# A one-core decode layer: the last weight row in two loads, the last projection's columns in two PSUM banks with a store each, and the residual put into the banks first

## The chip, the cores and the metric

The kernel runs on one core of a Trainium2 chip. The metric is the device time of one execution in microseconds. Three runs of the kernel before gave 137.87, 137.88 and 137.82 us, a median of 137.87 us.

## What is computed

One decode step of a transformer layer for a batch of four tokens: layer norm, attention over the last 2048 positions of a key and value cache (32 query heads on 4 key/value heads), an output projection with a residual, a second layer norm, a gated feed-forward network, and a second residual. Everything enters and leaves in bf16.

```python
# x 4x1x1024; k_cache, v_cache 4x4x8192x128; wq 1024x4096; wo 4096x1024
# w1, w3 1024x3584; w2 3584x1024
h = x + attention(layernorm(x), k_cache, v_cache, wq, wo)   # window: the last 2048 positions
n = layernorm(h)
gate = n @ w1
up = n @ w3
h2 = h + (silu(gate) * up) @ w2
return h2
```

## The kernel before

With four tokens there is little arithmetic for each weight, so the kernel is a stream of 55.6 MB out of HBM through a ring of 160 KB in each of the 128 partitions. `plan` is the list of loads in order: wq, the keys, the values, wo, w1, w3, w2. Each entry has a place in the ring. `load_next(n)` issues the next `n` of them on the sync engine's DMA queue (SP); where it is called in the program decides after which matmuls the issue may come, since a load overwrites ring space that earlier matmuls read.

A "row" of a weight is one slice of the contraction: partition p of `w2_v` holds the 28 rows of w2 that belong to it one behind the other, and `loaded["w2"][i]` is row i in all partitions, 128 x 1024 values, 256 KB. The 28 rows of w2 come in four loads: rows 0 to 16, 17 to 23 (`R1` = 17), 24 to 26 (`R2` = 24) and row 27. The last three are issued by `load_next(3)` within the w1 matmuls (line 467).

Matrix products put the four tokens in a small stationary operand, 32 columns wide, and stream the weights. The 1024 output columns are cut into `JG` = 4 column groups of `CG` = 256; group j has its results in PSUM partitions 32j to 32j+31 (`QD` = 32), of which every eighth (`RS` = 8) belongs to a token. Four matmuls, one for each group, run at the same time in different columns of the array.

The work around the change, in program order:

- wo (L411): 32 rows into `y_ps`. VectorE adds the residual (L424) and has `h1`, the layer's middle value, 128 x 256 in fp32.
- The second layer norm (L426 to L449): statistics of `h1` on VectorE, one matmul that adds them over the column groups (L433, `sums_ps`), a square root on ScalarE, and the normalised rows transposed to `hnT`.
- w1 and w3 (L459, in `gate_up`): 64 matmuls each into `g_ps` and `u_ps`, with the silu on ScalarE and VectorE between; `hgT` (L481) is the transposed product.
- w2 (L492, in `down`): rows 0 to 16 go into the bank of `y2_ps`, whole groups of 256 columns. When they are done, VectorE adds `h1` and has `h2` (L501). Rows 17 to 27 go into two other banks, `ya_ps` with the first 128 columns of each group and `yb_ps` with the second 128 columns. Behind row 23 two matmuls with the fp32 identity `ident_f` add `h2` into these banks (L507).
- The end: VectorE copies `ya_ps` to bf16 (L513), ScalarE copies `yb_ps` (L514), and one DMA, issued on ScalarE's queue, stores all four column groups (L515). L541 is the end of the program, where the engines wait for all transfers and for one another.

The tile framework places the waits and may order independent instructions of an engine; the order of the queues quoted below is that of the built program.

Of the kernel before, what the change touches and what calls it, by code (L numbers as in the profile page):

```python
# [10 lines left out]
P = 128  # L11
ACT = mybir.ActivationFunctionType
ALU = mybir.AluOpType
AX = mybir.AxisListType
BF16 = mybir.dt.bfloat16
FP32 = mybir.dt.float32
# [3 lines left out]
def kernel(  # L20
# [13 lines left out]
    nc = tc.nc  # L34

    B, _, D = A_x.shape
# [13 lines left out]
    out_flat = out.flatten_outer_dims()  # L50
# [8 lines left out]
    wide = ctx.enter_context(tc.tile_pool(name="wide", bufs=2))  # L59
    const = ctx.enter_context(tc.tile_pool(name="const", bufs=1))  # L60
    act = ctx.enter_context(tc.tile_pool(name="act", bufs=1))
# [3 lines left out]
    JG = 4  # L65
    QD = P // JG
    RS = QD // B
    CQ = Hq * Dh // JG
    CG = D // JG
# [3 lines left out]
    IF = F // P  # L73
# [5 lines left out]

    RING = 5 * 16384  # L80
    R1, R2 = 17, 24
    RQ = 4
    BS = 2
    wq_v = A_wq.rearrange("(p i) n -> p (i n)", i=KC)
# [3 lines left out]
    w2_v = B_w2.rearrange("(p i) n -> p (i n)", i=IF)  # L88
    ring = stream.tile([P, RING], BF16)
# [33 lines left out]
    def load_tail(at, src, n, r0, m):  # L123

        t = ring[:, at : at + m * n]
        nc.sync.dma_start(out=t[:, : m * n - CE], in_=src[:, r0 * n : (r0 + m) * n - CE])
        return [t[:, k * n : (k + 1) * n] for k in range(m)]
    KIB = 512
    plan = [
        ("wq", load_rows, (0, wq_v, N_Q, 0, 4)),  # L130
        ("side", load_side, SETS[0]),
        ("side", load_side, SETS[1]),
        ("wq", load_tail, (32 * KIB, wq_v, N_Q, 4, 4)),
        ("k", load_kv, (64 * KIB, A_k_cache, 0)),
        ("k", load_kv, (96 * KIB, A_k_cache, 2)),
        ("v", load_kv, (128 * KIB, A_v_cache, 0)),
        ("v", load_kv, (0, A_v_cache, 2)),
        ("wo", load_rows, (32 * KIB, wo_v, D, 0, 32)),
        ("w1", load_rows, (96 * KIB, w1_v, N_F, 0, 8)),
        ("w3", load_rows, (0, w3_v, N_F, 0, 8)),  # L140
        ("w2", load_rows, (56 * KIB, w2_v, D, 0, 17)),
        ("w2", load_rows, (90 * KIB, w2_v, D, 17, 7)),
        ("w2", load_rows, (104 * KIB, w2_v, D, 24, 3)),
        ("w2", load_rows, (110 * KIB, w2_v, D, 27, 1)),
    ]
    loaded = {}
    cursor = [0]

    def load_next(n=1):
        for _ in range(n):  # L150
            if cursor[0] < len(plan):
                kind, f, args = plan[cursor[0]]
                loaded.setdefault(kind, []).extend(f(*args))
                cursor[0] += 1
# [13 lines left out]
    for c in range(2):  # L168
        nc.sync.dma_start(
            out=x_q[c * 2 * QD : (c + 1) * 2 * QD : RS, :],  # L170
            in_=x_flat.rearrange("b (j c) -> j b c", j=JG)[2 * c : 2 * c + 2],
# [7 lines left out]
    for c in range(2):  # L179
# [8 lines left out]
        out=xn[:], in0=x_sb[:], scalar1=mv[:, 0:1], scalar2=rstd[:, 0:1],  # L188
# [14 lines left out]
    for r0, ne, ns in SETS:  # L203
# [3 lines left out]
            out=xs[:, len(sl) : len(sl) + ns, : ne * 4].rearrange("b l (i s) -> b l i s", s=4),  # L207
            in_=v[:, KC - 1, :, :, :],
        )
        for l in range(ns):  # L210
            nc.tensor.transpose(
                out=ts_ps[: ne * 4, len(sl), :], in_=xs[:, len(sl), : ne * 4], identity=ident[:B, :B]
# [4 lines left out]
    for _, ne, ns in SETS:  # L217
# [9 lines left out]
    ident_f = const.tile([P, P], FP32)  # L227
# [4 lines left out]
        out=perm[:].rearrange("p (h dq) -> p h dq", dq=JG),  # L232
        in_=ident[:].rearrange("p (dq h) -> p h dq", dq=JG),
# [12 lines left out]
    for j in range(2, JG):  # L246
        nc.vector.tensor_tensor(
            out=same[:, 0, :], in0=same[:, 0, :], in1=ident[:, j * QD : (j + 1) * QD], op=ALU.add
# [6 lines left out]
    for kc in range(KC):  # L255
        wq_t = loaded["wq"][kc]
        for hf in range(CQ // 512):
            for g in range(JG):
                c0 = g * CQ + hf * 512
                n = min(512, N_Q - CE - c0) if kc == KC - 1 else 512  # L260
                if n <= 0:
# [3 lines left out]
                    lhsT=xnT[:, kc, :],  # L265
                    rhs=wq_t[:, c0 : c0 + n],
                    start=(kc == 0),
                    stop=(kc == KC - 1 or (kc == KC - 2 and c0 + 512 == N_Q)),
                )
        if kc == RQ - 1:  # L270
            load_next()
            for k, np_ in enumerate(sl):
                nc.tensor.matmul(
                    q_ps[QD * (JG - 1) : QD * (JG - 1) + B, CQ - CE : CQ],
                    lhsT=xsT[:np_, k, :],
                    rhs=loaded["side"][k],
                    start=False,
                    stop=False,
# [5 lines left out]
    for r in range(REP):  # L284
        nc.tensor.transpose(out=qt_ps[:, r, :], in_=q_sb[:, r * Dh : (r + 1) * Dh], identity=ident[:])
    nc.vector.tensor_copy(
        out=qz[:, :, : Hkv * QD].rearrange("p b (g z) -> p b g z", g=Hkv)[:, :, :, :REP],
        in_=qt_ps[:].rearrange("p r (g x) -> p x g r", g=Hkv)[:, :B, :, :],
# [24 lines left out]
    for u, (b, n) in enumerate(units):  # L313
        k_v = loaded["k"][b]
        kT = ktpool.tile([P, NJ, P], BF16, tag="kT")
        for t in range(NJ // TB):
            kt_ps = psA.tile([P, TB, P], BF16, tag=f"kt{nt % 4}")
            for jj in range(TB):
                nc.tensor.transpose(  # L319
                    out=kt_ps[:, jj, :], in_=k_v[:, n * NJ + t * TB + jj, :], identity=ident[:]  # L320
# [21 lines left out]
        out=Pm[:], in_=scores_ps[:], func=ACT.Exp, bias=nmax[:], scale=1.0, accum_out=rsum[:]  # L342
# [6 lines left out]
    for c in range(NSB):  # L349
# [4 lines left out]
        for g in range(Hkv):  # L354
            if g % 2 == 0:
                nc.vector.tensor_scalar(  # L356
                    out=z[:, :, g, :], in0=pt_ps[:], scalar1=mask[:, g : g + 1], scalar2=None, op0=ALU.mult
# [10 lines left out]
        out=Dm[:], in0=ident[:].rearrange("p (g b r) -> p b g r", g=Hkv, b=B),  # L368
# [11 lines left out]
    for b in range(B):  # L380
        for j in range(JK):
            nc.tensor.matmul(  # L382
                OT_ps[:, b, :],
                lhsT=loaded["v"][b][:, j, :],
                rhs=PTz[j // NJ][:, (j % NJ) * B + b, :, :],
                start=(j == 0),
                stop=(j == JK - 1),
# [13 lines left out]

    psB = ctx.enter_context(tc.tile_pool(name="psB", bufs=1, space=bass.MemoryType.PSUM))
    y_ps = psB.tile([P, CG], FP32, tag="y")
    HC = CG // 2
    ya_ps = psB.tile([P, 512], FP32, tag="ya")
    yb_ps = psB.tile([P, 512], FP32, tag="yb")
    g_ps = psB.tile([P, 2, 512], FP32, tag="g")
    u_ps = psB.tile([P, 2, 512], FP32, tag="u")
    for i in range(IO):
        for j in range(JG):  # L410
            nc.tensor.matmul(  # L411
                y_ps[QD * j : QD * (j + 1), :],
                lhsT=o4[:, i, :, :].rearrange("p b s -> p (b s)"),
                rhs=loaded["wo"][i][:, j * CG : (j + 1) * CG],
                start=(i == 0),
                stop=(i == IO - 1),
# [6 lines left out]
    h1 = act.tile([P, CG], FP32)  # L423
# [20 lines left out]
        out=hn[:], in0=h1[:], scalar1=tot[:, 0:1], scalar2=rstd2[:, 0:1],  # L444
# [5 lines left out]
        out=hnT[:].rearrange("p k x -> p (k x)"), in_=hn[:].rearrange("q (c k) -> q k c", k=KC)  # L450
# [3 lines left out]
    def gate_up(kind, out_ps):  # L454
        for k in range(KC):
            for hf in range(2):
                for j in range(JG):
                    c0 = j * CF + hf * HF
                    nc.tensor.matmul(  # L459
                        out_ps[QD * j : QD * (j + 1), hf, :HF],  # L460
                        lhsT=hnT[:, k, :],
                        rhs=loaded[kind][k][:, c0 : c0 + HF],
                        start=(k == 0),
                        stop=(k == KC - 1),
                    )
            if kind == "w1" and k == RQ - 1:
                load_next(3)

    gate_up("w1", g_ps)
    eg = wide.tile([P, 2, HF], FP32, tag="w4k")  # L470
    nc.scalar.activation(out=eg[:], in_=g_ps[:, :, :HF], func=ACT.Exp, scale=-1.0)
    nc.vector.tensor_scalar_add(out=eg[:], in0=eg[:], scalar1=1.0)
    nc.vector.reciprocal(out=eg[:], in_=eg[:])  # L473
    gs = wide.tile([P, 2, HF], FP32, tag="w4k")
    nc.vector.tensor_tensor(out=gs[:], in0=g_ps[:, :, :HF], in1=eg[:], op=ALU.mult)
    gate_up("w3", u_ps)
    hg = act.tile([P, 2, HF], BF16)
    nc.vector.tensor_tensor(out=hg[:], in0=u_ps[:, :, :HF], in1=gs[:], op=ALU.mult)
# [3 lines left out]
        out=hgT[:].rearrange("p i x -> p (i x)"),  # L482
        in_=hg[:].rearrange("q s c -> q (s c)").rearrange("q (c i) -> q i c", i=IF),
    )


    y2_ps = psB.tile([P, CG], FP32, tag="y")
    h2 = wide.tile([P, CG], FP32, tag="w4k")

    def down(i, n, c0, out_ps, **kw):  # L490
        for j in range(JG):
            nc.tensor.matmul(  # L492
                out_ps[QD * j : QD * (j + 1), :n],
                lhsT=hgT[:, i, :],
                rhs=loaded["w2"][i][:, j * CG + c0 : j * CG + c0 + n],
                **kw,
            )

    for i in range(R1):
        down(i, CG, 0, y2_ps, start=(i == 0), stop=(i == R1 - 1))  # L500
    nc.vector.tensor_tensor(out=h2[:], in0=y2_ps[:], in1=h1[:], op=ALU.add)  # L501
    for i in range(R1, IF):
        for c, t in enumerate((ya_ps, yb_ps)):
            down(i, HC, c * HC, t, start=(i == R1), stop=(i == IF - 1), skip_group_check=True)
        if i == R2 - 1:
            for c, t in enumerate((ya_ps, yb_ps)):
                nc.tensor.matmul(  # L507
                    t[:, :HC], lhsT=ident_f[:], rhs=h2[:, c * HC : (c + 1) * HC],
                    start=False, stop=False, skip_group_check=True,
                )  # L510

    res = act.tile([P, CG], BF16)
    nc.vector.tensor_copy(out=res[:, :HC], in_=ya_ps[:, :HC])  # L513
    nc.scalar.copy(out=res[:, HC:], in_=yb_ps[:, :HC])  # L514
    nc.scalar.dma_start(out=out_flat.rearrange("b (j c) -> j b c", j=JG), in_=res[0:P:RS, :])  # L515


# [28 lines left out]
```

## Time and profile before

| what | value |
| --- | --- |
| median of three runs | 137.87 us |
| profiled execution, span of the core | 136.0 us |
| its mean granted TensorE clock | 0.720 |
| HBM read | 55.59 MB, 409 GB/s over the span |
| TensorE matmuls busy | 72.3 us (53%) |
| VectorE busy | 43.9 us (32%) |
| ScalarE busy | 31.0 us (23%) |
| chain that ended last: DMA | 54% |
| chain that ended last: TensorE | 25% |

Busy time is the time in which an engine worked on instructions other than waits and DMA issues. The chain that ended last is followed backward from the last instruction, at each step to what released it; its lines give a start, a duration and the engine or transfer that the step went through. In the timeline a line gives start, duration, engine, line of the kernel, the operation with output and input, and in brackets how long the engine stood before it and for what. The weights' rows of the timeline that have a count (x4) are merged: the duration is that of the whole group, from the first start to the last end. In the rows by stretch the granted clock is 1.0 at full speed. "Landing" is the moment at which a transfer's completion is seen.

### The profile page before, as it was taken

The page shows a single profiled execution, that of the slowest core. Times are in us where ns is not written, and L with a number is a line of the kernel's source. Part 1 is how long each engine was busy: PE and PEld are TensorE (multiplying, and loading weights), DVE is VectorE, ACT ScalarE, POOL GpSimd, SP SyncE. Part 2 cuts the span into 40 slices and gives each one's busy share as a digit, 9 for nine tenths or more (in the row PEclk, how much of TensorE's full clock was granted, in tenths as well). Part 3 has the DMA queues.
Part 4 walks back from the last instruction along what each step waited for, and adds up shares of the span by engine and source line. Part 5 has one row for each costly group of instructions (what it writes and reads, how often), then busy time and mean ns, then how long its engine had stood idle before and what let it go on. Part 6 is the DMA issues. An engine that isn't in the chain of part 4 may idle for free.

```text
span 136.0 us, 2436 instructions
## 1 busy us (share of the span) xinstructions
PE 72.3 (53%) x1096; PEld 46.1 (34%) x1096; DVE 43.9 (32%) x79; ACT 31.0 (23%) x36; POOL 1.7 (1%) x8
## 2 busy tenths in 40 slices
PE   0004920979898989810525916791097000970981
PEld 0002300268374756500014905570043000430870
DVE  5055000043344444470994001206200596026010
ACT  3000000015555555609294300000001400000000
POOL 5000000000000000000000000000000000000000
PEclk9999975557999999985555555568556855568568
DMA  5999999999999999999989999989989899999970
GB/s 155 464 463 406 412 420 414 429 424 439 424 439 424 424 443 426 410 552 453 463 347 463 463 410 405 477 354 494 439 371 494 371 472 401 399 420 407 424 298 5
DMA packets 2650, 55.75 MB, mean 410 GB/s; under 512 B 296, under 2 KB 464, under 8 KB 720
## 3 DMA queue, kind: packets, MB, share of 16 engines
q1 hardware_dynamic: 2604, 55.58, 95.6%
q8 instruction: 8, 0.13, 0.3%
q10 hardware_dynamic: 36, 0.02, 0.0%
q14 instruction: 2, 0.02, 0.0%
HBM read 55.59 MB, written 0.01 MB: 409 GB/s over the span
## 4 chain that ended last, share of the span: by engine, by line
DMA 54%; PE 25%; ACT 11%; DVE 5%; SPq 2%; issue 1%; ACTq 0%
DMA ring<-in_B_w_dram 38%; DMA ring<-in_A_wq_dram 15%; PE kt_ps L319 11%; ACT kT L325 5%; PE scores_ps L304 5%; ACT z L360 3%; PE q_ps L263 3%; DVE rmax L336 2%; ACT Pm L341 2%; PE OT_ps L382 2%; DVE pT L350 1%; SPq L120 1%; PE g_ps L459 1%; DVE z L356 1%; ACT L341 1%
## 5 line engine op out<-in xcount | busy, mean ns | idle before, releaser
L325 ACT COPY kT<-kt_ps 128x1024 bf16<-128x1024 bf16 x16 | 15.9, 1013 | 13.4 <-PE kt_ps L319 13.4
L319 PE MATMUL kt_ps<-ident,ring 128*128 128x128 bf16 x256 | 18.0, 232 | 0.0
L319 PEld LDWEIGHTS <-ring 128*128 128x128 bf16 x256 | 16.0, 105 | 4.9 <-issue 4.9
L323 DVE COPY kT<-kt_ps 128x1024 bf16<-128x1024 bf16 x16 | 11.1, 692 | 16.5 <-PE kt_ps L319 16.5
L459 PEld LDWEIGHTS <-hnT 128*32 128x32 bf16 x128 | 5.5, 143 | 21.8 <-issue 19.2
L382 PE MATMUL OT_ps<-z,ring 128*128 128x32 bf16 x256 | 7.5, 188 | 8.5 <-ACT z L360 5.0
L459 PE MATMUL u_ps<-ring,hnT 128*32 128x448 bf16 x64 | 6.0, 563 | 11.0 <-DMA ring<-in_B_w_dram 11.0
L304 PE MATMUL scores_ps<-kT,qz 128*32 128x512 bf16 x64 | 9.9, 609 | 2.9 <-ACT kT L325 2.9
L263 PE MATMUL q_ps<-ring,xnT 128*4 128x512 bf16 x63 | 6.7, 595 | 7.8 <-DMA ring<-in_A_wq_dram 7.8
L382 PEld LDWEIGHTS <-ring 128*128 128x128 bf16 x256 | 7.4, 104 | 9.2 <-issue 9.2
L459 PE MATMUL g_ps<-ring,hnT 128*32 128x448 bf16 x64 | 5.9, 558 | 4.9 <-DMA ring<-in_B_w_dram 4.9
L492 PEld LDWEIGHTS <-hgT 128*32 128x32 bf16 x156 | 4.9, 134 | 6.2 <-issue 5.7
L411 PE MATMUL y_ps<-ring,o 128*32 128x256 bf16 x128 | 5.9, 371 | 0.8 <-DVE o L398 0.8
L514 ACT CAST res<-yb_ps 128x128 bf16<-128x128 f32 x1 | 0.3, 266 | 26.1 <-PE yb_ps L492 26.1
L492 PE MATMUL y_ps<-ring,hgT 128*32 128x256 bf16 x68 | 3.8, 419 | 4.4 <-DMA ring<-in_B_w_dram 4.4
L360 ACT ACTIVATE z<-pt_ps,mask 128x512 bf16<-128x512 f32 x8 | 5.3, 687 | 3.5 <-DVE z L356 3.5
L352 PE MATMUL pt_ps<-pT,perm 128*128 128x512 bf16 x4 | 2.4, 607 | 6.8 <-DVE pT L350 6.8
L263 PEld LDWEIGHTS <-xnT 128*4 128x4 bf16 x63 | 2.0, 115 | 11.7 <-issue 11.6
L194 PE MATMUL tp_ps<-ident,xn 4*128 4x4 bf16 x8 | 0.7, 200 | 10.0 <-DVE xn L187 10.0
L356 DVE TENSOR_SCALAR z<-pt_ps,mask 128x512 bf16<-128x512 f32 x8 | 5.5, 741 | 1.2 <-ACT z L360 0.8
L473 DVE RECIPROCAL eg<-eg 128x896 f32<-128x896 f32 x1 | 5.8, 5753 | 0.0
L411 PEld LDWEIGHTS <-o 128*32 128x32 bf16 x128 | 4.4, 131 | 3.1 <-DVE o L398 1.9
(85 smaller groups left out, 50.1 us busy)
## 6 DMA issues: line engine op xcount, KB each, us to landing
ring<-in_B_w_dram SPq DMA_DIRECT2D x2, 7168.0 KB, 22.5
ring<-in_A_k_cache_dram SPq DMA_DIRECT2D x4, 2048.0 KB, 27.6
ring<-in_A_v_cache_dram SPq DMA_DIRECT2D x4, 2048.0 KB, 29.2
ring<-in_B_w_dram SPq DMA_DIRECT2D x1, 4352.0 KB
ring<-in_A_wq_dram SPq DMA_DIRECT2D x1, 4096.0 KB, 12.2
ring<-in_A_wq_dram SPq DMA_DIRECT2D x1, 3968.0 KB
ring<-in_B_w_dram SPq DMA_DIRECT2D x1, 1792.0 KB
ring<-in_B_w_dram SPq DMA_DIRECT2D x1, 768.0 KB
```

The source lines that it names most:

```text
L263: nc.tensor.matmul(q_ps[QD * g : QD * g + B, hf * 512 : hf * 512 + n], lhsT=xnT[:, kc, :], rhs=wq_t[:, c0 : c0 + n], start=(kc == 0), stop ...
L304: nc.tensor.matmul(scores_ps[QD * g : QD * (g + 1), n * 512 : (n + 1) * 512], lhsT=qz_v[:, z0 : z0 + QD], rhs=kT_v[:, g, :, :], start=(b = ...
L319: nc.tensor.transpose(out=kt_ps[:, jj, :], in_=k_v[:, n * NJ + t * TB + jj, :], identity=ident[:])
L323: nc.vector.tensor_copy(out=kT[:, t * TB : (t + 1) * TB, :], in_=kt_ps[:])
L325: nc.scalar.copy(out=kT[:, t * TB : (t + 1) * TB, :], in_=kt_ps[:])
L356: nc.vector.tensor_scalar(out=z[:, :, g, :], in0=pt_ps[:], scalar1=mask[:, g : g + 1], scalar2=None, op0=ALU.mult)
L360: nc.scalar.mul(out=z[:, :, g, :], in_=pt_ps[:], mul=mask[:, g : g + 1])
L382: nc.tensor.matmul(OT_ps[:, b, :], lhsT=loaded["v"][b][:, j, :], rhs=PTz[j // NJ][:, (j % NJ) * B + b, :, :], start=(j == 0), stop=(j == J ...
L411: nc.tensor.matmul(y_ps[QD * j : QD * (j + 1), :], lhsT=o4[:, i, :, :].rearrange("p b s -> p (b s)"), rhs=loaded["wo"][i][:, j * CG : (j + ...
L459: nc.tensor.matmul(out_ps[QD * j : QD * (j + 1), hf, :HF], lhsT=hnT[:, k, :], rhs=loaded[kind][k][:, c0 : c0 + HF], start=(k == 0), stop=( ...
L473: nc.vector.reciprocal(out=eg[:], in_=eg[:])
L492: nc.tensor.matmul(out_ps[QD * j : QD * (j + 1), :n], lhsT=hgT[:, i, :], rhs=loaded["w2"][i][:, j * CG + c0 : j * CG + c0 + n], **kw,)
```

## The change

Row 27 of w2 is loaded in two pieces by a new function: column groups 0 to 2 (192 KB), then group 3 (64 KB); `JL` = 3. All four remaining loads of w2's tail are issued at the place where three were. The two banks no longer hold halves of each group: `y2_ps` holds groups 0 to 2 whole, `y2b_ps` group 3. All 28 rows accumulate in them, with matmuls of 256 columns. `h1` is added first: two identity matmuls of 256 columns open the two accumulations before w1's matmuls in the program (in the built order ahead of the statistics matmul L433 in TensorE's queue, behind wo's matmuls). `h2` and its VectorE addition go. At the end VectorE copies groups 0 to 2 (96 partitions x 256), and the sync queue stores them; ScalarE copies group 3 (32 partitions x 256), and its queue stores that. Only the last row's fourth matmul waits for the second piece.

```diff
+    JL = JG - 1
...
+    def load_last(at, j0, j1):
+
+        t = ring[:, at : at + D]
+        r0 = (IF - 1) * D
+        nc.sync.dma_start(out=t[:, j0 * CG : j1 * CG], in_=w2_v[:, r0 + j0 * CG : r0 + j1 * CG])
+        return [t]
+
...
-        ("w2", load_rows, (104 * KIB, w2_v, D, 24, 3)),
-        ("w2", load_rows, (110 * KIB, w2_v, D, 27, 1)),
+        ("w2", load_rows, (104 * KIB, w2_v, D, R2, IF - 1 - R2)),
+        ("w2", load_last, (110 * KIB, 0, JL)),
+        ("w2b", load_last, (110 * KIB, JL, JG)),
...
-    HC = CG // 2
-    ya_ps = psB.tile([P, 512], FP32, tag="ya")
-    yb_ps = psB.tile([P, 512], FP32, tag="yb")
+    y2_ps = psB.tile([P, CG], FP32, tag="ya")
+    y2b_ps = psB.tile([P, CG], FP32, tag="yb")
...
-                load_next(3)
-
+                load_next(4)
+
+    for t in (y2_ps, y2b_ps):
+        nc.tensor.matmul(t[:], lhsT=ident_f[:], rhs=h1[:], start=True, stop=False, skip_group_check=True)
     gate_up("w1", g_ps)
...
-    y2_ps = psB.tile([P, CG], FP32, tag="y")
-    h2 = wide.tile([P, CG], FP32, tag="w4k")
-
-    def down(i, n, c0, out_ps, **kw):
+    for i in range(IF):
         for j in range(JG):
+            if i == IF - 1 and j == JL:
+                w = loaded["w2b"][0]
+            else:
+                w = loaded["w2"][i]
             nc.tensor.matmul(
-                out_ps[QD * j : QD * (j + 1), :n],
+                (y2b_ps if j == JL else y2_ps)[QD * j : QD * (j + 1), :],
                 lhsT=hgT[:, i, :],
-                rhs=loaded["w2"][i][:, j * CG + c0 : j * CG + c0 + n],
-                **kw,
+                rhs=w[:, j * CG : (j + 1) * CG],
+                start=False,
+                stop=(i == IF - 1),
+                skip_group_check=True,
             )
 
-    for i in range(R1):
-        down(i, CG, 0, y2_ps, start=(i == 0), stop=(i == R1 - 1))
-    nc.vector.tensor_tensor(out=h2[:], in0=y2_ps[:], in1=h1[:], op=ALU.add)
-    for i in range(R1, IF):
-        for c, t in enumerate((ya_ps, yb_ps)):
-            down(i, HC, c * HC, t, start=(i == R1), stop=(i == IF - 1), skip_group_check=True)
-        if i == R2 - 1:
-            for c, t in enumerate((ya_ps, yb_ps)):
-                nc.tensor.matmul(
-                    t[:, :HC], lhsT=ident_f[:], rhs=h2[:, c * HC : (c + 1) * HC],
-                    start=False, stop=False, skip_group_check=True,
-                )
-
-    res = act.tile([P, CG], BF16)
-    nc.vector.tensor_copy(out=res[:, :HC], in_=ya_ps[:, :HC])
-    nc.scalar.copy(out=res[:, HC:], in_=yb_ps[:, :HC])
-    nc.scalar.dma_start(out=out_flat.rearrange("b (j c) -> j b c", j=JG), in_=res[0:P:RS, :])
+    out_v = out_flat.rearrange("b (j c) -> j b c", j=JG)
+    res = wide.tile([P, CG], BF16, tag="w4k")
+    resb = wide.tile([P, CG], BF16, tag="w4k")
+    nc.vector.tensor_copy(out=res[: QD * JL, :], in_=y2_ps[: QD * JL, :])
+    nc.sync.dma_start(out=out_v[:JL], in_=res[0 : QD * JL : RS, :])
+    nc.scalar.copy(out=resb[QD * JL :, :], in_=y2b_ps[QD * JL :, :])
+    nc.scalar.dma_start(out=out_v[JL], in_=resb[QD * JL : P : RS, :])
```

## The prediction

> **What bounds the kernel now.** I read the chain of waits first. Its last two long links are transfers, and all that follows is short:
>
> ```profile
> 100.48 29.74 DMA ring<-in_B_w_dram
> 130.22 0.04 issue
> 130.27 0.30 PE ya_ps L492 x3
> ...
> 131.82 0.42 PE ya_ps L507 x2
> 132.24 0.22 PE yb_ps L507 x2
> ...
> 133.06 0.02 issue
> 133.08 0.27 ACT res L514
> ```
>
> To 130.22 the kernel is weight streaming (the page gives 409 GB/s of HBM reads over the span). The change touches none of the 55.6 MB, so it acts on what lies behind 130.22 only: 5.8 of the 136.0 us.
>
> In that tail I asked when the last two loads of w2 (three rows, one row) are there. The list of DMA issues and the sync queue's issues (start, duration) say:
>
> ```profile
> ring<-in_B_w_dram SPq DMA_DIRECT2D x1, 256.0 KB, 31.3
> 101.34 0.42 SPq L94 DMA_DIRECT2D ring<-in_B_w_dram  x1
> ```
>
> The one-row load lands at 101.34 + 31.3 = 132.64. The sync queue's closing waits, in order of time, place the load before it: after its last issue (101.34 + 0.42 = 101.76) it waits for transfers three times, in total
>
> ```profile
> SPq L541 <- DMA ring<-in_B_w_dram: 30.2, 3, 24.2
> ```
>
> so the third, for the three-row load, ends at about 101.76 + 30.2 + the gaps between = 132.1. Now the timeline of TensorE (start, duration, operation):
>
> ```profile
> 131.75 0.49 PE L507 MATMUL ya_ps<-h,ident_f 128*128 128x128 f32 x2
> 132.08 0.39 PE L507 MATMUL yb_ps<-h,ident_f 128*128 128x128 f32 x2
> 132.39 0.24 PE L492 MATMUL ya_ps<-ring,hgT 128*32 128x128 bf16 x4
> 132.79 0.23 PE L492 MATMUL yb_ps<-ring,hgT 128*32 128x128 bf16 x4
> 133.02 0.29 DVE L513 CAST res<-ya_ps 128x128 bf16<-128x128 f32 x1 [2.67 <-PE yb_ps L492]
> 133.08 0.27 ACT L514 CAST res<-yb_ps 128x128 bf16<-128x128 f32 x1 [26.10 <-PE yb_ps L492]
> 133.39 0.64 ACTq L515 DMA_DIRECT2D out_dram<-res  x1
> ```
>
> This is the view that decides. TensorE has no gap from 130.27 on: it fills the wait for the three rows with the residual's matmuls (131.75 to 132.39). From 132.39 on, eight groups of four follow each other, two to a row and 0.055 apart; the last row's two start at about 132.74 and 132.79, and its data are there at 132.64. So TensorE reaches the last row only 0.1 us after it has landed. Taking the residual matmuls away can't bring more than that, because the data would then be late. The store is issued from 133.39 to 134.03; the sync queue's wait for it (1.8 us, ending the work) ends at 133.39 + 1.79 = 135.18, 1.15 after the end of the issue. The 0.82 us to 136.0 are closing barriers that stay.
>
> **The change part by part.** All sums are against this execution; 137.87 - 136.0 = 1.87 us lie outside its span and stay.
>
> *The residual moves to the front.* L501 (0.42) and two L507 matmuls go from the tail; two of twice the width come in ahead of the layer norm's sums matmul in TensorE's queue, as the built order shows. In the tail this is worth at most the 0.1 us above. In front it costs: two 128-column ones took 131.75 to 132.39 = 0.64 at a granted clock of 1.0, so two 256-column ones take at most 1.28 at that clock, 2.6 at half. They wait for h1, which ends at 92.41:
>
> ```profile
> 91.99 0.42 DVE L424 TENSOR_TENSOR h<-y_ps,x_q 128x256 f32<-128x256 f32 x1 [6.08 <-PE y_ps L411]
> 93.53 0.38 PE L433 MATMUL sums_ps<-mv,same 128*128 128x2 f32 x2 [1.66 <-DVE mv L431]
> 96.19 0.10 PEld L459 LDWEIGHTS <-hnT 128*32 128x32 bf16 x1 [2.36 <-DVE hnT L449]
> 98.80 5.87 PE L459 MATMUL g_ps<-ring,hnT 128*32 128x448 bf16 x64 [4.88 <-DMA ring<-in_B_w_dram]
> ```
>
> The granted clock there is 1.00 to 94.0 and 0.50 after, so they end at 92.46 + 1.28 = 93.7, and the sums matmul, with the whole norm behind it, is 0.2 late; at half clock all through, they end at 95.0 and it is 1.5 late. The cover is the w1 load: TensorE has hnT at 96.19 and stands until w1 lands at 98.76, 2.6 us. Cost nothing; without that cover 0.2 to 1.5.
>
> *Seven and three rows in one bank pair.* 256 columns at once instead of two times 128: the streamed columns are the same (one row of four took 0.107 at full clock, 0.213 at half). The seven rows stay 130.27 to 131.75. Then TensorE now waits for the three rows: 132.1 + 0.05 (from landing to first matmul, as 130.22 to 130.27) + 3 x 0.107 = 132.47. It is done before the last row lands, so no gain passes through here.
>
> *Last row in two loads.* One more issue on the sync queue, 0.42, at 101.8, 30 us ahead of need and with nothing behind it but the closing waits: nothing. The bytes: from 131.60 to 131.80 the 2 KB packets moved 256 GB/s at a busy share of 0.67, which is 25 packets in 2.14 engine-us, 86 ns each; the store's 512 B packets made 56 GB/s at 0.21 from 134.70 to 134.80, 11 packets in 0.34, 31 ns each. Eight packets of 512 B on each of 16 engines take 0.25, a quarter of eight of 2 KB 0.17. So the second load lands 0.08 later than the whole row did, 132.72, and the first about 0.2 before it, 132.5. Bounds for the second's delay: 0 (bytes alone count) to 0.6 (it starts only when the first is complete: its own 0.25, and 0.33 from last byte to landing as for the store, busy to 134.85 and there at 135.18). I take 0.08, from the rows nearest in packet size, since the load is queued 30 us before its turn.
>
> *Column group 4: matmul, copy, store.* Start 132.72 + 0.05 = 132.77. A 256-column matmul at full clock took 0.27 (the shortest of L411): 133.04. ScalarE's start 0.06 behind: 133.10. Its copy of 256 columns lies between 0.27 (128, L514) and 0.60 (512, L282); on the line 0.38: 133.48. Store issue at 133.52, 0.13 later than before. The issue of a plain four-row transfer on this queue (x_sb) took 0.27 and 0.56, that of the old 16-row store 0.64: 0.42 taken, ends 133.94, lands 1.15 later: 135.09.
>
> *Groups 1 to 3.* First part there at 132.5, matmuls 132.55 to 132.82, VectorE at 132.87, 0.42 for 256 columns (L501's row): 133.30. The sync queue issues at 133.34. Behind this wait stand the closing waits alone, most already satisfied. The issue of an 8-row transfer there (x_q) took 0.54: ends 133.88, lands 135.03. Both stores are needed; the later is 135.09, 0.09 before 135.18. One more closing wait costs 0.03 (L541's median 28 ns).
>
> Sum: -0.09 + 0.03 = -0.06 us, so **137.8 us**. Bounds of the parts: issues of 0.27 and 0.33 (a plain sync-queue load) give -0.25; no saving in the issue (0.64), the copy at 0.60 and the second load 0.6 late give -0.06 + 0.22 + 0.22 + 0.52 = +0.9.
>
> The Trainium skill speaks against this edit: "DMA: Bandwidth & Descriptors", section "Bandwidth", holds that transfers under 64 KB are mostly descriptor overhead, and its table gives 0.95 us for 64 KB; if the 64 KB load behaved so, an estimate is 0.95 - 0.17 = 0.8 us later and 138.6. No run here shows a lone load of that size; the packets of this trace decide for me.
>
> The clock matters too. In the half-microsecond rows it is 0.50 to 131.5, 0.95 to 132.0, then 1.00. Were the step half a microsecond later, the old tail, which has no gap, would do that half at half speed and end about 0.25 later; the new one waits for data and loses at most 0.05. Were it earlier, the old tail would gain the 0.1 it has and stop at the data. So the clock can only help the change; I put no term on it. The skill's "TensorE: Matmul & The Clock Gate", section "What's actually happening", says that the window which decides the clock runs free of the kernel, so that the step would fall elsewhere in each execution; by it the median could hold some hundredths more gain than my sum, but one profile can't show that.
>
> **Rivals.**
> 1. *The stores were what cost* (faster). The old store is one 3-dimensional issue of 0.64; each new one is smaller. If both issues take about 0.3 and fewer packets land sooner, the old 133.39 to 135.18 shrinks by 0.35 to 0.4, which outweighs +0.13 on ScalarE. For it: x_sb's 0.27. Against: the sync queue's own 3-dimensional issue of 0.54. With 0.35 + 0.15 for fewer packets (the store's were busy from 134.66 to 134.85) less 0.13: 137.5.
> 2. *The 64 KB load's own completion* (slower). One mechanism: the second load lands as a transfer of its own, not as the tail of the row. Everything in the last column group is serial behind it, so each 0.1 counts in full; from 0.35 us late on (0.27 over my 0.08) it makes the kernel over 0.2% slower. For it: the store's 0.33 between bytes and landing. Against: the old row landed 0.24 after its last bytes (DMA traffic ends by 132.4) and that is already in 132.64. At 0.5 us late: 138.2.
> 3. *It does something else than it says.* The two banks could be shared, which would make VectorE's copy and the last matmuls meet; the built program gives each its own, so this has almost no weight: 0.01. The copy would then start only behind the last matmul (133.04 for 132.82), 0.2 later on the earlier chain: 138.0, slower still if both stores then queue.
>
> **How the numbers follow.** 0.2% of 137.87 is 0.28 us, about what a measurement of this kernel tells from no change. The even trade has 0.56 (137.6 to 138.1), rival 1 0.23, rival 2 0.20, rival 3 0.01. The range leaves about a tenth at either end: 137.45 to 138.25. Faster 0.23, same 0.56, slower 0.21.
>
> **What would show it.** In the new profile: w1's first matmul still starts at 98.8 behind the load, with the sums matmul up to 0.7 later; TensorE has a gap of about 0.35 before the three rows and another before the last group; ScalarE's copy starts near 133.1 and takes 0.38; VectorE's ends near 133.3; the two store issues are 0.3 to 0.6. I am wrong if the second load lands after 133.0, if either store lands more than 0.28 away from 135.18, or if w1's matmuls start late.

## The result, and the profile after

The changed kernel takes 138.45 us (median of 5 runs, 138.35 to 138.57) against 137.82 us for the kernel before beside it: a ratio of 1.0044, 95% interval 1.0032 to 1.0056. It is 0.6 us slower, where 137.8 was forecast and 137.45 to 138.25 given as the range. A second measurement, with 23 runs of the kernel before, gave 1.004 (1.0027 to 1.0052). The profiled execution has a span of 136.7 us, against 136.0.

The chain of waits of the changed kernel still ends in two long transfers, so the kind of bound is the same (columns: start, duration, step):

```profile
74.34 24.63 DMA ring<-in_B_w_dram
98.97 0.04 issue
99.01 2.12 PE g_ps L467 x20
101.13 31.11 DMA ring<-in_B_w_dram
132.24 0.04 issue
132.29 0.29 PE y_ps L503 x3
```

In the profile before it led through the seven-row load; here it leads through the three-row load (132.24), since TensorE has nothing left to fill that wait with. The old tail isn't without a gap in every execution, though. In a second profile of the kernel before the clock stepped up at 129.90 and not at 131.55; there TensorE stood for the three rows even behind its residual matmuls, and then for the last row, so the 0.1 us that the prediction allowed for these matmuls wasn't there:

```profile
131.45 0.39 PE L507 MATMUL yb_ps<-h,ident_f 128*128 128x128 f32 x2
132.06 0.24 PE L492 MATMUL ya_ps<-ring,hgT 128*32 128x128 bf16 x4 [0.23 <-DMA ring<-in_B_w_dram]
```

The end of the changed kernel, in the timeline:

```profile
130.44 0.40 PE L503 MATMUL y_ps<-ring,hgT 128*32 128x256 bf16 x3 [0.46 <-DMA ring<-in_B_w_dram]
...
132.76 0.29 PE L503 MATMUL y_ps<-ring,hgT 128*32 128x256 bf16 x3
132.94 0.27 PE L503 MATMUL y2b_ps<-ring,hgT 128*32 128x256 bf16 x1
133.09 0.42 DVE L515 CAST res<-y_ps 96x256 bf16<-96x256 f32 x1 [9.86 <-PE y_ps L503]
133.25 0.36 ACT L517 CAST resb<-y2b_ps 32x256 bf16<-32x256 f32 x1 [25.88 <-PE y2b_ps L503]
133.54 0.79 SPq L516 DMA_DIRECT2D out_dram<-res  x1
133.64 0.70 ACTq L518 DMA_DIRECT2D out_dram<-resb  x1
```

The two pieces of the last row arrive apart: their matmuls start at 132.76 and 132.94. The copies are 256 columns wide and take 0.42 and 0.36, where the old ones took 0.29 and 0.27. Both store issues are longer than the old one (0.79 and 0.70 against 0.64) and run at the same time. The rows by stretch (TensorE, its loads, VectorE, ScalarE, GpSimd, then granted clock, share of the DMA engines, GB/s) show the two stores' bytes apart from each other:

```profile
134.95:135.10 0.15, 0.00 (x0) 0.00 (x0) 0.00 (x0) 0.00 (x0) 0.00 (x0) 1.00 0.15 41
135.10:135.25 0.15, 0.00 (x0) 0.00 (x0) 0.00 (x0) 0.00 (x0) 0.00 (x0) 1.00 0.00 0
135.25:135.35 0.10, 0.00 (x0) 0.00 (x0) 0.00 (x0) 0.00 (x0) 0.00 (x0) 1.00 0.09 21
```

The issues end at 134.33 and 134.35; the first store's bytes come 0.64 later, much as before (0.63), but the second's only at 135.26, 0.3 behind the first's and 0.91 behind the end of their own issue. The sync queue's closing waits for the landings (count, shortest/median/longest ns, first and last start) are these in the changed kernel:

```profile
L544 SPq EVENT_SEMAPHORE  x2: 28/635/1242, 134.4 to 134.4; - x2
L544 SPq EVENT_SEMAPHORE  x3: 28/28/28, 135.7 to 135.8; - x3
```

The long one begins at 134.45 (134.4 in the view) and ends with the later landing, 1.24 on, at 135.69. Three more short waits follow it one after another. In the kernel before, the wait that ends with the landing at 135.18 is the last of them. The queue takes these waits in the same order in every profile here, so the wait for the last landing can stand at the end of the row or earlier in it. Step by step, from the profiled executions:

| step | before | after | difference |
| --- | --- | --- | --- |
| seven rows: first matmul | 130.27 | 130.44 | +0.17 |
| store issue begins (the later) | 133.39 | 133.64 | +0.25, so 0.08 more |
| that issue's duration | 0.64 | 0.70 | +0.06 |
| end of that issue to landing | 1.15 | 1.34 | +0.19 |
| landing to the end of the span | 0.82 | 0.98 | +0.16 |
| span | 136.0 | 136.7 | +0.66 |

### The profile page after: what moved, and what is told of

Its sections match the earlier page's. It is cut to its first block, busy times and chain, and to the rows that moved or that the text cites. A ratio compares the mean times of both kernels' runs of the same rounds, so it can differ in the third digit from the quotient of the medians.

```text
span 136.7 us, 2349 instructions
## 1 busy us (share of the span) xinstructions
PE 69.7 (51%) x1052; PEld 43.9 (32%) x1052; DVE 43.7 (32%) x78; ACT 31.0 (23%) x36; POOL 1.7 (1%) x8
## 4 chain that ended last, share of the span: by engine, by line
DMA 56%; PE 21%; ACT 13%; DVE 5%; SPq 2%; issue 1%; ACTq 0%
DMA ring<-in_B_w_dram 41%; DMA ring<-in_A_wq_dram 15%; PE kt_ps L328 9%; ACT kT L334 6%; PE scores_ps L313 5%; ACT z L369 3%; PE q_ps L272 2%; DVE rmax L345 2%; PE g_ps L467 2%; ACT Pm L350 2%; PE OT_ps L391 1%; DVE pT L359 1%; SPq L121 1%; DVE z L365 1%; ACT L350 1%
## 5 line engine op out<-in xcount | busy, mean ns | idle before, releaser
L328 PE MATMUL kt_ps<-ident,ring 128*128 128x128 bf16 x256 | 16.5, 219 | 0.0
L328 PEld LDWEIGHTS <-ring 128*128 128x128 bf16 x256 | 14.4, 98 | 5.0 <-issue 4.9
L391 PEld LDWEIGHTS <-ring 128*128 128x128 bf16 x256 | 7.4, 104 | 8.8 <-issue 8.8
L467 PE MATMUL u_ps<-ring,hnT 128*32 128x448 bf16 x64 | 4.5, 448 | 10.8 <-DMA ring<-in_B_w_dram 10.8
L503 PE MATMUL y_ps<-ring,hgT 128*32 128x256 bf16 x84 | 6.3, 398 | 6.4 <-DMA ring<-in_B_w_dram 6.4
L503 PE MATMUL y2b_ps<-ring,hgT 128*32 128x256 bf16 x28 | 6.3, 398 | 0.0
```

The costliest lines, as they stand in the source:

```text
L328: nc.tensor.transpose(out=kt_ps[:, jj, :], in_=k_v[:, n * NJ + t * TB + jj, :], identity=ident[:])
L391: nc.tensor.matmul(OT_ps[:, b, :], lhsT=loaded["v"][b][:, j, :], rhs=PTz[j // NJ][:, (j % NJ) * B + b, :, :], start=(j == 0), stop=(j == J ...
L467: nc.tensor.matmul(out_ps[QD * j : QD * (j + 1), hf, :HF], lhsT=hnT[:, k, :], rhs=loaded[kind][k][:, c0 : c0 + HF], start=(k == 0), stop=( ...
L503: nc.tensor.matmul((y2b_ps if j == JL else y2_ps)[QD * j : QD * (j + 1), :], lhsT=hgT[:, i, :], rhs=w[:, j * CG : (j + 1) * CG], start=Fal ...
```

## The experiments

My theory after this: the two stores hurt each other at their issue. The rivals: the 64 KB load and what is serial behind it; the weight stream itself, 0.17 late already at the seven rows; the early residual. Each experiment was timed with the kernel before beside it; times below are medians, with the ratio to that kernel and its 95% interval.

### The two kernels again

No edit; for a second profile of each.

> The changed kernel a second time, as the measure of the others on this chip: 138.3 to 138.6 us. Theory (two stores): its two store issues again take 0.7 to 0.8 us each, and the one on ScalarE's queue lands about 2.0 us after its issue, against 1.79 before. Rival (the weight stream itself is late): the seven-row load of w2 lands again near 130.40, 0.2 later than in the profile of before. If it lands at 130.2 here, that 0.2 was chance.

> The kernel before once more, for a second profile of its stream: 137.75 to 137.9. If the landing of the seven-row load of w2 moves by 0.1 to 0.2 from 130.22 while the time stays, the shift seen in the changed kernel is the spread of single executions; if it stands at 130.2, the changed kernel's stream is late by itself.

Changed: 138.52, 1.004 (1.0027 to 1.0052). Before: 137.85, 0.9998 (0.9989 to 1.0006). The first matmul of the seven rows stood at 130.28 in the changed kernel's second profile (130.44 in the first) and at 130.23 in before's (130.27). In the other kernels below it stood between 130.23 and 130.40 whatever their edit; the mean is 130.35 over the six profiles whose kernel has the change's early residual and adds all 28 rows to it, and 130.33 over the other eight. So the 0.17 of the table is mostly the spread of single executions; the late stream falls as a cause. One expectation missed: in the changed kernel's second profile it was the sync queue's store that landed late, 2.17 after its issue began, and ScalarE's took 1.8.

### The changed kernel with parts undone

One store in place of two (`res` now holds all four groups):

```diff
-    nc.sync.dma_start(out=out_v[:JL], in_=res[0 : QD * JL : RS, :])
-    nc.scalar.copy(out=resb[QD * JL :, :], in_=y2b_ps[QD * JL :, :])
-    nc.scalar.dma_start(out=out_v[JL], in_=resb[QD * JL : P : RS, :])
+    nc.scalar.copy(out=res[QD * JL :, :], in_=y2b_ps[QD * JL :, :])
+    nc.scalar.dma_start(out=out_flat.rearrange("b (j c) -> j b c", j=JG), in_=res[0:P:RS, :])
```

> The changed kernel with one store on ScalarE's queue for all four groups behind both copies; split load, banks and early residual stay. Theory (two stores collide: 0.26 us from issue to landing and about 0.15 more of closing waits): 0.4 us less than the changed kernel, 138.0 to 138.1. Rival (split load and the late stream): at most 0.1 less, 138.35 or more.

Measured: 138.09, 1.0012 (1.0004 to 1.0021), 0.43 less than the changed kernel beside it. As the theory said, though of the 0.15 that it booked for the closing waits only 0.06 came back (0.92 from the landing to the end, against 0.98). The timeline, with the issue short again:

```profile
132.90 0.27 PE L503 MATMUL y2b_ps<-ring,hgT 128*32 128x256 bf16 x1
133.06 0.42 DVE L513 CAST res<-y_ps 96x256 bf16<-96x256 f32 x1 [9.53 <-PE y_ps L503]
133.21 0.36 ACT L514 CAST res<-y2b_ps 32x256 bf16<-32x256 f32 x1 [27.23 <-PE y2b_ps L503]
133.60 0.66 ACTq L515 DMA_DIRECT2D out_dram<-res  x1
```

One load in place of two for row 27:

```diff
-        ("w2", load_last, (110 * KIB, 0, JL)),
-        ("w2b", load_last, (110 * KIB, JL, JG)),
+        ("w2", load_rows, (110 * KIB, w2_v, D, IF - 1, 1)),
...
-                load_next(4)
+                load_next(3)
```

> The changed kernel with row 27 in one load; two stores, banks and early residual stay. Theory (two stores): 0.1 us less at most, 138.35 to 138.45. Rival (the 64 KB load and what is serial behind it): 0.3 us or more less, 138.15 or under.

Measured: 138.53, 1.0042 (1.0029 to 1.0054), no different from the changed kernel. The rival of the 64 KB load falls as the cause of the loss.

Both undone:

> Both undone: what is left of the change is the early residual and the banks by column groups, with copies of 256 columns. Theory: 137.95, that is before plus the 0.1 us by which a 256-column copy on ScalarE is longer. If the early residual or the order of the banks delays the stream: 138.1 or more. If neither costs and the residual's absence from the tail gains: 137.8 or less.

Measured: 138.08, 1.001 (1.0001 to 1.0019), between the two forecasts and the same as with one store alone. Some 0.17 us are left that neither the second store nor the split load makes. In the timelines they lie whole between the first matmul of the last row and the store's issue: 132.81 to 133.64 here, 0.83, and 132.70 to 133.36 in the second profile of the kernel before, 0.66.

That the split load alone makes no difference has two sides. With one store it brings the store's issue forward, to 3.20 us behind the seven rows' first matmul against 3.29 undivided. But it also lengthens the end: from the landing to the end of the span it is 0.92 with the split load and 0.82 without, because two closing waits then stand behind the wait for the store (the kernel with one store, from 135.43 on):

```profile
L541 SPq EVENT_SEMAPHORE  x2: 28/28/28, 135.5 to 135.5; - x2
```

### The kernel before with one part added

Two stores, both behind both copies:

```diff
-    nc.scalar.dma_start(out=out_flat.rearrange("b (j c) -> j b c", j=JG), in_=res[0:P:RS, :])
+    out_v = out_flat.rearrange("b (j c) -> j b c", j=JG)
+    JL = JG - 1
+    nc.sync.dma_start(out=out_v[:JL], in_=res[0 : QD * JL : RS, :])
+    nc.scalar.dma_start(out=out_v[JL], in_=res[QD * JL : P : RS, :])
```

> The kernel before, with the one store cut into groups 0 to 2 on the sync queue and group 3 on ScalarE's, both behind both copies. Theory (two stores collide): 0.3 to 0.45 us slower, 138.15 to 138.3, each issue 0.7 to 0.8 us. Rival (the stores cost nothing, the split load does): 137.85, within 0.1 of before.

Measured: 138.33, 1.0038 (1.0026 to 1.005), +0.42. That is two thirds of the change's loss from the stores alone, and the same 0.43 that the changed kernel gets back without them. The timeline and the stretches in which their bytes move:

```profile
133.47 0.79 SPq L517 DMA_DIRECT2D out_dram<-res  x1
133.47 0.71 ACTq L518 DMA_DIRECT2D out_dram<-res  x1
```

```profile
134.80:134.95 0.15, 0.00 (x0) 0.00 (x0) 0.00 (x0) 0.00 (x0) 0.00 (x0) 1.00 0.06 14
134.95:135.15 0.20, 0.00 (x0) 0.00 (x0) 0.00 (x0) 0.00 (x0) 0.00 (x0) 1.00 0.00 0
135.15:135.35 0.20, 0.00 (x0) 0.00 (x0) 0.00 (x0) 0.00 (x0) 0.00 (x0) 1.00 0.12 31
```

Issued in the same hundredth, their bytes are 0.36 apart. Here ScalarE's went first; in the changed kernel's first profile the sync queue's did, in its second ScalarE's: each time the one whose issue ended first. The three-group store landed 2.19 after its issue began, and from there to the end it took 0.92, against 1.79 and 0.82 with the one store.

The split load:

```diff
-        ("w2", load_rows, (110 * KIB, w2_v, D, 27, 1)),
+        ("w2", load_last, (110 * KIB, 0, JG - 1)),
+        ("w2b", load_last, (110 * KIB, JG - 1, JG)),
...
-                rhs=loaded["w2"][i][:, j * CG + c0 : j * CG + c0 + n],
+                rhs=loaded["w2b" if i == IF - 1 and j == JG - 1 else "w2"][0 if i == IF - 1 and j == JG - 1 else i][
+                    :, j * CG + c0 : j * CG + c0 + n
+                ],
```

> The kernel before with row 27 in two loads of 192 and 64 KB; the last row's fourth group waits for the second. Theory (two stores): 0.05 to 0.15 us slower by its packets, 137.9 to 137.97. Rival (a load of its own, late to complete): 0.3 us or more slower, 138.15.

Measured: 138.06, 1.001 (1.0002 to 1.0019): +0.15, at the upper edge of the theory's difference and half of the rival's. From the seven rows' first matmul to the last piece's it took 2.55, and in the changed kernel 2.50; undivided rows took 2.46 to 2.47 in three profiles (before again, one load, both undone). So the second piece is 0.03 to 0.09 late. In this kernel both copies wait for it, so nothing comes back, and the store is issued 3.17 behind the seven rows' first matmul, against 3.11 to 3.13 in the kernels with the old tail up to there. The larger part is at the end: 0.92 from the landing to the end of the span in place of 0.82, again with two closing waits behind the store's.

The early identity matmuls, added to the kernel before with their result overwritten:

```diff
+    for t in (ya_ps, yb_ps):
+        nc.tensor.matmul(t[:, :CG], lhsT=ident_f[:], rhs=h1[:], start=True, stop=True, skip_group_check=True)
     gate_up("w1", g_ps)
```

> The kernel before plus the two early identity matmuls of the change; their result is overwritten when rows 17 to 27 open the two banks, and the residual is still added in the tail. It prices the early residual's place alone. Theory (hidden under the wait for w1): before within 0.1 us, 137.8 to 138.0, the sums matmul at most 0.2 to 1.5 later and w1's first matmul unchanged. Rival (the early matmuls delay the norm or the stream): 138.1 or more.

Measured: 137.96 beside 137.93, 1.0002 (0.9993 to 1.0011). The early residual is free. The timeline shows why, with the sums matmul right behind the new ones and 4.6 us between hnT's first use and the load that w1 waits for:

```profile
91.17 0.59 PE L470 MATMUL yb_ps<-h,ident_f 128*128 128x256 f32 x2
91.70 0.39 PE L433 MATMUL sums_ps<-mv,same 128*128 128x2 f32 x2
...
94.36 0.09 PEld L459 LDWEIGHTS <-hnT 128*32 128x32 bf16 x1 [2.36 <-DVE hnT L449]
98.97 0.94 PE L459 MATMUL g_ps<-ring,hnT 128*32 128x448 bf16 x8 [6.88 <-DMA ring<-in_B_w_dram]
```

### What in the pair costs

The one store on the sync queue, then two stores of two groups each, then three groups and one behind each other on ScalarE's queue:

```diff
-    nc.scalar.dma_start(out=out_flat.rearrange("b (j c) -> j b c", j=JG), in_=res[0:P:RS, :])
+    nc.sync.dma_start(out=out_flat.rearrange("b (j c) -> j b c", j=JG), in_=res[0:P:RS, :])
```

> The kernel before with its one store on the sync queue in place of ScalarE's. Theory (two issues at one moment slow each other): the lone issue takes 0.55 to 0.65 us there too, lands about 1.8 after its issue, and the time is that of before, within 0.15 us: 137.75 to 138.0. Rival (the sync queue is a slow place for a store, so the 0.79 us issue is its own): 0.79 us again and 138.05 or more.

Measured: 137.89 beside 137.96, 0.9998 (0.9989 to 1.0007). The issue took 0.65. The sync queue is no slower a place for a store.

```diff
-    JL = JG - 1
+    JL = 2
...
-    nc.scalar.dma_start(out=out_v[JL], in_=res[QD * JL : P : RS, :])
+    nc.scalar.dma_start(out=out_v[JL:], in_=res[QD * JL : P : RS, :])
```

> The kernel before with two stores of two column groups each, on the sync queue and ScalarE's. Theory (collision of the issues, whatever their shape): 138.3, as with three groups and one. Rival (the uneven cut of three and one is what costs): 138.05 or less.

Measured: 138.18, 1.0017 (1.0008 to 1.0026): +0.22, between the two forecasts, so both were half right. The issues took 0.60 and 0.64, the lone store's time, and the bytes were 0.36 apart all the same:

```profile
134.70:134.85 0.15, 0.00 (x0) 0.00 (x0) 0.00 (x0) 0.00 (x0) 0.00 (x0) 1.00 0.10 27
134.85:135.05 0.20, 0.00 (x0) 0.00 (x0) 0.00 (x0) 0.00 (x0) 0.00 (x0) 1.00 0.00 0
135.05:135.20 0.15, 0.00 (x0) 0.00 (x0) 0.00 (x0) 0.00 (x0) 0.00 (x0) 1.00 0.10 27
```

The second store landed at 135.54, 2.06 after its issue began, where the lone one took 1.79: 0.27 for the meeting. The uneven cut adds the longer issue, 0.79 for three groups against 0.60 for two, and 0.10 behind the last landing: 0.92 there, but 0.82 here, where the wait for the store that lands last is the last of the closing waits.

```diff
-    nc.sync.dma_start(out=out_v[:JL], in_=res[0 : QD * JL : RS, :])
+    nc.scalar.dma_start(out=out_v[:JL], in_=res[0 : QD * JL : RS, :])
```

> The kernel before with the stores of three groups and one both on ScalarE's queue, one behind the other. If the cost of the pair is that the two issues go through something they share, one queue is little worse than two: the second is issued 0.6 later and 138.3 to 138.5. If the two queues hurt each other by running at once and one queue would not: each issue 0.5 to 0.64 and the packets of the second right behind its issue, but the serial issue alone makes it 138.4 or more. A time of 138.2 or less would say that only the queues' meeting costs.

Measured: 138.87, 1.0069 (1.0055 to 1.0083), within the 138.4 or more of the expectation's second case. In a row they are slower still: the two issues end 1.56 behind the start of the first, where the lone one takes 0.64:

```profile
133.50 0.87 ACTq L517 DMA_DIRECT2D out_dram<-res  x1
134.42 0.65 ACTq L518 DMA_DIRECT2D out_dram<-res  x1
```

Three groups took 0.87 here with no other queue busy, above the 0.5 to 0.64 expected, so the long issue belongs to that store and not to the meeting. Nor is the second store's start delayed when the two issues end 0.69 apart: its bytes come 0.64 behind the end of its own issue (135.07), as a lone store's do:

```profile
135.00:135.20 0.20, 0.00 (x0) 0.00 (x0) 0.00 (x0) 0.00 (x0) 0.00 (x0) 1.00 0.12 31
135.20:135.65 0.45, 0.00 (x0) 0.00 (x0) 0.00 (x0) 0.00 (x0) 0.00 (x0) 1.00 0.00 0
135.65:135.85 0.20, 0.00 (x0) 0.00 (x0) 0.00 (x0) 0.00 (x0) 0.00 (x0) 0.61 0.05 10
```

### The early residual without the rest

All 28 rows into two banks of column halves, copies of 128 columns, one load, one store:

```diff
+    for i in range(IF):
+        for c, t in enumerate((y2_ps, y2b_ps)):
+            for j in range(JG):
+                nc.tensor.matmul(
+                    t[QD * j : QD * (j + 1), :HC],
+                    lhsT=hgT[:, i, :],
+                    rhs=loaded["w2"][i][:, j * CG + c * HC : j * CG + (c + 1) * HC],
+                    start=False,
+                    stop=(i == IF - 1),
+                    skip_group_check=True,
+                )
```

> The early residual alone: all 28 rows into the two banks of column halves, copies of 128 columns on VectorE and ScalarE, one load, one store. Theory: TensorE waits for the last row, so the gain is the 0.1 us or less that the kernel before reaches it late: 137.75 to 137.85. If the residual in the tail did cost (a later clock step in most executions): 137.6 or less. If the early one delays the stream: 138.0.

Measured: 138.27 (137.96 to 138.87), 1.0034 (1.002 to 1.0049). None of the three forecasts. The timeline shows a stop of TensorE inside the seven rows, whose data are there:

```profile
130.94 0.23 PE L502 MATMUL y_ps<-ring,hgT 128*32 128x128 bf16 x2
132.43 0.23 PE L502 MATMUL y_ps<-ring,hgT 128*32 128x128 bf16 x2 [1.26 <-issue]
```

"Issue" means that it waited for nothing the profile names. This kernel has 68 matmuls more than the kernel before. A 16 KB transfer of instructions ended at 131.09, just before the stop, but every other kernel here has one between 130.3 and 132.0 too; this one alone has a further one, at 133.55. Whether TensorE waited for its instructions wasn't tried. What the early residual can bring to the tail is left open by this run.

None of the versions beats the kernel before.

## Why the prediction was wrong

The step that failed is "Column group 4: matmul, copy, store", in its last term, and with it "Groups 1 to 3". I priced the two store issues at 0.42 and 0.54 from x_sb's and x_q's loads, let each land 1.15 after its own issue, and took the later of two independent stores, 135.09. They are not independent, and not short:

- The issue of ScalarE's store took 0.70 (+0.28 on 0.42), of the sync queue's 0.79 (+0.25). The four-row store is no shorter than the old sixteen-row one at 0.64; the fewer rows saved nothing. The load that I took the price from was the wrong row: the old store itself was the nearest.
- The end of the issue to the landing was 1.34 in place of 1.15 (+0.19): the second store's bytes started 0.91 behind the end of its issue in place of 0.63.
- The closing waits were put at +0.03, the length of one wait; the span after the landing grew by 0.16 (+0.13 on the forecast). What counts is how many waits stand behind the one for the last landing: none, two or three gave 0.82, 0.92 and 0.98. This part is not the stores' alone, since the split load by itself makes 0.92.

Together that is 0.60 too little. The steps up to the later store's issue were put 0.05 too high (+0.13, and +0.08 from the seven rows on), so this profile's tail is 0.49 longer where -0.06 was forecast. The table's other 0.17 is the start of the seven rows, which the runs don't show to be the change's. That the medians still lie 0.6 apart fits the executions in which the three-group store lands last: in the kernel with one load, as slow as the changed one, seven rows to end took 6.32 against 5.73 before, +0.59.

Counted from the one old store rather than from my price, the pair costs 0.37 to 0.40 up to the last landing when the three-group store is last (2.16 to 2.19 from issue to landing in three profiles, against 1.79), and up to 0.10 of closing waits; the two experiments on it say +0.42 when added, -0.43 when removed. The forecast had moreover booked a gain of 0.22 for a shorter issue (0.64 to 0.42) that didn't exist. The sign of error that the prediction named did show: the later store landed at 135.69, 0.51 from 135.18.

Two sums of the prediction are off without touching its forecast: its lowest case, with the closing wait that the sum adds, is -0.21 and not -0.25; and by its own terms the second load has to be 0.42 late, not 0.35, to make the kernel 0.28 slower.

The other steps held:

- *Early residual*: nothing forecast, +0.03 measured and inside the interval.
- *Seven and three rows*: no gain passes, since TensorE waits. The gap before the three rows is there: 0.15 in the first profile, 1.16 in the second.
- *Last row in two loads*: the second piece 0.08 late forecast, 0.03 to 0.09 seen; the first 0.14 early forecast, 0.09 to 0.14 seen (2.37 with the split load alone and 2.32 in the changed kernel, against 2.46 from the seven rows). Its closing waits, 0.10, had no price. The figure of 0.95 us for 64 KB from the Trainium skill's "DMA: Bandwidth & Descriptors", section "Bandwidth", which is measured there on transfers issued from GpSimd, does not describe a load on the sync queue that is queued behind others: the second piece followed the first by 132.94 - 132.76 = 0.18 here.
- *Copies of 256 columns*: 0.38 and 0.42 forecast, 0.36 and 0.42 seen. With 0.13 more on VectorE this is the likeliest part of the 0.17 that remains without second store and split load; it is read from the timeline and was not tried alone.

Of the rivals, the second had the right sign with the wrong mechanism: it put the loss into the load, which was in time. The third mentioned in its last words, for the case of shared banks, that both stores could queue, but gave it no price and a chance of 0.01. That was where the time went. The upper bound for the issues was 0.64 each, the old store's time, which alone gives 138.0; no term stood for their meeting, and the 0.9 of all upper bounds together was cut to 138.25 by the chances.

## What to carry to other kernels

The last store is a serial chain of issue, way to the engines, bytes, landing and closing waits. Here 8 KB took 1.79 us from issue to landing, and 2 KB behind another store on the same queue 1.74, so a smaller piece saves next to nothing. Cutting the store in two lets one part start earlier, but the end waits for the later part, whose chain was no shorter, and two issues at one moment cost 0.2 to 0.4. Issues that ended 0.69 apart did not delay each other; how far apart they must be on two queues was not tried. Price a new DMA issue from the nearest issue of the same direction and shape, not from loads on its queue, and count for every added transfer the closing waits that then stand behind the last landing, about 0.05 each here.

## What the runs showed of the hardware

- Two small stores issued together on two queues started their bytes 0.30 to 0.36 us apart (five profiles in all: the changed kernel twice, one load, two stores uneven and even). The first was each time the one whose issue ended first. A lone store, or the first of the two, started them 0.63 to 0.65 behind the end of its issue on either queue. What they share is not shown by these runs.
- A store of three column groups took 0.79 to 0.87 us to issue, of one, two or four groups 0.60 to 0.71. Two, three and four were run on both queues, one on ScalarE's alone.
- From the last landing to the end of the span it took 0.82 us when the wait for that landing was the last of the sync queue's closing waits (seven profiles), 0.92 with two behind it (six) and 0.98 with three (one).
- TensorE without its filler can lose its clock. In the second profile of the changed kernel it had been granted full clock early, stood for the three-row load, and fell to half just as the rows arrived (rows by stretch, granted clock third from the right):

```profile
131.25:132.30 1.05, 0.00 (x0) 0.00 (x0) 0.00 (x0) 0.00 (x0) 0.00 (x0) 0.99 0.69 241
132.30:133.30 1.00, 0.91 (x16) 0.50 (x15) 0.00 (x0) 0.00 (x0) 0.00 (x0) 0.50 0.04 12
```

That execution's span was 137.0. Its clock had stepped up at 128.88. In the kernel before with two stores it stepped up at 128.89, the residual's matmuls filled the wait, and full clock held to 135.71. The stretch of full clock up to the point where one lost it, first without and then with the filler, has TensorE busy for 1.50 and for 2.34 of 3.41 us:

```profile
128.88:132.29 3.41, 1.50 (x48) 1.11 (x41) 0.00 (x0) 0.00 (x0) 0.00 (x0) 1.00 0.84 333
128.89:132.30 3.41, 2.34 (x91) 1.94 (x84) 0.42 (x1) 0.00 (x0) 0.00 (x0) 1.00 0.84 340
```

In the profiles here the step to full clock before the tail came at anything from 128.9 to 132.1, in agreement with the Trainium skill's "TensorE: Matmul & The Clock Gate", section "What's actually happening", that the deciding window runs free of the kernel; the prediction had said that the clock could only help the change, and this execution shows that it can also hurt it.
